# Numerators as 32x32 products, key-value sums in column tiles, and a layer norm by quarters in a four-layer attention kernel

## The chip, the cores and the metric

The kernel runs on one core of a Trainium2 chip. Its engines work side by side and meet through semaphores: TensorE multiplies matrices (PE in the profile; its loads of stationary matrices are PEld), VectorE (DVE) and ScalarE (ACT) work elementwise, GpSimd (POOL) does a little here, and SyncE (SP) mostly issues transfers. Products land in PSUM, eight banks of 512 fp32 columns over 128 partitions; everything else lies in SBUF.

The metric is the device time of one execution in microseconds, given as the median over the runs.

## The reference

Four layers follow each other: A, B, A, B, with the same weights for both A and both B. There are 2048 rows of 1024, and 32 heads of 32.

```
x = x + A(layernorm(x)); x = x + B(layernorm(x))      # and once more
A:  pq, pk = q @ w_phi, k @ w_phi                      # per head, 32x32
    phi_q = [softmax(pq), softmax(-pq)]                # 64 features per head, phi_k alike
    kv  = sum over s of phi_k[s,f] * v[s,d];  z = sum over s of phi_k[s,f]
    o   = (phi_q @ kv) / (phi_q @ z + 1e-6);  return o @ wo
B:  p = softmax(q k^T * 32**-0.5);  return (p @ v) @ wo
```

A is a linear attention: its keys are summed up once into a 32x32 matrix per head and sign, and its queries are multiplied with these. B is an ordinary attention over 2048 x 2048 scores per head.

## The kernel before

The activations stay in SBUF, transposed, as `xT`: 1024 features in eight blocks of 128 partitions, 2048 rows in four chunks of 512. Each pair of layers A and B is one turn of a loop (`layer` 0 and 1) with these stages:

- **Keys of A** (`a_keys`, L595 on). For each chunk: a layer norm (`layernorm`, L468 on), then for each half of the heads (`fc`) four blocks of 128 rows. A block has a product for the keys and one for the values, two exponentials (L615), their sums (L619), a reciprocal (L622), and the values multiplied by it into 33 columns per head, the last one holding the reciprocal itself (L628, L633). After four blocks the sums over rows follow (L647): for each of eight pairs of head group and sign, four products that contract the rows, with 128 stationary columns (four heads) and 132 moving ones (four heads of 33). Only the four diagonal blocks of 32x33 are wanted; they are added to an accumulator in SBUF by four DVE instructions for each of three banks of results (L662, L665).
- **State** (`a_state`). The accumulator is laid out for the queries: a block diagonal `kvm` of 128x128 per head group and sign, cleared by POOL (L688) and filled by four DVE copies (L692), and a matrix `zm` for the denominators from `zz` (L694, L700, L702).
- **Query pass of A** (`a_queries`, L734 on, and `a_out`). For each chunk and half: the query products, exponentials (L745), sums over features by small column tiles (L756), a correction of the negative half spread over heads by `spread` (L728, stationary `selb`), then for each of four head groups `a` the numerators (L783: two products of 128x128 by 512, for the two signs) copied out by ACT (L787), the denominators in column tiles (L794), their reciprocal by logarithm and exponential (L799, L801), spread again by `selb`, and multiplied in (L805). `a_out` multiplies by `wo` and adds to `xT` (L818). Then the chunk's layer norm for B follows, and B's keys of the first head group (`b_k`, evacuated at L841, moved by DMA at L834) and values.
- **Attention of B** (`attention`). Score products (L1009) use four row tiles of 32 partitions, three at a time into three banks; ACT takes the exponential of 1536 columns at once (L1017); the products with the values and with ones (L1047) use four column tiles. Some exponentials are made on DVE (L952 to L969). The projections of other head groups and the output projection run beside it as filler in bank 7 (L428), with column tiles. Towards the end of layer 0's attention the keys of layer 1's A for chunks 0 to 2 run there too (`alone`), with SBUF copies and bank 7 in place of free banks. Idle products (L1265) fill gaps.

The order of the work is not written out by hand. `Sched` collects every operation with its engine, an assumed duration, its dependencies, its buffers and a priority, then runs a list schedule over the engines and emits the instructions in that order; each engine's queue is in order. Buffers come from classes with a quota (`QUOTA`), and are given out in order of priority within a class; PSUM banks of class "num" have a quota of one. Each PE operation carries a mode that tells the array's shape: "n" for the whole array, "c" for column tiles, "r" for row tiles.

Layer norms outside attention square `xT` on ACT in two halves (L480), or in four quarters where `n=4`, and sum values and squares by products with a matrix of 1/1024 (L424); evacuations (L500, L502), the variance (L503), its logarithm and exponential (L505, L507) and four pairs of DVE instructions (L513, L517) follow. With two halves the squares and the sums wait for the whole chunk of `xT`; with quarters each waits for its two blocks. In the kernel before, only the first layer norm of layer 1 has `n=4`.

`gate` is an empty list: the first score product of an attention waits for its operands alone.

```
gate = []                                            # L1188
so = op("PE", 0.24, sfn, deps + (gate if n == 0 else []), ...)
```

Of the kernel before, what the change touches and what calls it, by code (L numbers as in the profile page):

```python
# [11 lines left out]
ALU = mybir.AluOpType  # L12
# [244 lines left out]
QUOTA = {"pk": 3, "pv": 2, "kv": 1, "ln": 2, "mm": 2, "cmp": 2, "bc": 4, "num": 1, "wt": 4, "fil": 2,  # L257
# [28 lines left out]
def kernel(  # L286
# [43 lines left out]
    selb = const.tile([P, P], BF16, tag="selb")  # L330
    fold = const.tile([P, DH], F32, tag="fold")
# [28 lines left out]
    )  # L360
    nc.vector.reduce_sum(out=hl[:], in_=fold[:, 4:8], axis=AX.X)
# [53 lines left out]
    def csl(c):  # L415
        return slice(c * C512, (c + 1) * C512)
# [50 lines left out]

    def layernorm(c, prio, banks, alone=False, n=2):  # L468
# [23 lines left out]
        m = mmgroup(mb, mv, lambda po: onesD[:], lambda po: xT[:, po, csl(c)], (), parts if n == 4 else [deps_x(c)] * 4, [], prio)  # L492
        q = mmgroup(qb, qv, lambda po: onesD[:], lambda po: xv()[:, po, :], [m],
# [34 lines left out]


# [65 lines left out]
    def a_keys(c, base, wk_s, wv_s, kv, banks, alone=False, step=0.1):  # L595
        xb, xv, fin = xnA[c]
        kv_b, kv_v, kv_last = kv
        for fc in range(2):
# [39 lines left out]
            for lo, hi in ((0, 3), (3, 6), (6, 8)):  # L638
                pr = base + step * (4 * fc + 3) + 1.5 * step
                pb, pv = ps("fil" if alone else "kv", banks)  # L640
                last = None
                for i in range(lo, hi):
                    gi, s = divmod(i, 2)

                    def fn(i=i, gi=gi, s=s, lo=lo, pv=pv, es=es, vs=vs):
                        for t in range(TB):
                            nc.tensor.matmul(  # L647
                                pv()[:, (i - lo) * 132:(i - lo + 1) * 132],
                                lhsT=es[t][1]()[:, s, gi * P:(gi + 1) * P],
                                rhs=vs[t][1]()[:, s, 4 * gi:4 * gi + 4, :].rearrange("p a b -> p (a b)"),  # L650
                                start=(t == 0), stop=(t == TB - 1))
                    last = op("PE", TB * 0.1, fn, [last] + flat([v[2] for v in vs]) + flat([e[2] for e in es]),
                              [pb] + [e[0] for e in es] + [v[0] for v in vs], pr, mode="n")
                adds = []
                for jj in range(4):
                    js = slice(32 * jj, 32 * jj + 32)
                    i0, i1 = 8 * fc + lo, 8 * fc + hi

                    def diag(pv=pv, js=js, jj=jj, n=hi - lo):
                        return pv()[js, 0:n * 132].rearrange("p (i x) -> p i x", x=132)[:, :, 33 * jj:33 * jj + 33]  # L660
                    if c == 0:
                        adds.append(op("DVE", dve_us(33 * (hi - lo)), lambda js=js, i0=i0, i1=i1, diag=diag: nc.vector.tensor_copy(  # L662
                            out=kv_v()[js, i0:i1, :], in_=diag()), [last], [pb, kv_b], pr))
                    else:
                        adds.append(op("DVE", dve_us(33 * (hi - lo)), lambda js=js, i0=i0, i1=i1, diag=diag: nc.vector.tensor_tensor(  # L665
                            out=kv_v()[js, i0:i1, :], in0=kv_v()[js, i0:i1, :], in1=diag(), op=ALU.add),
                            flat([last, kv_last.get((fc, lo))]), [pb, kv_b], pr))
                kv_last[(fc, lo)] = adds
# [13 lines left out]
    def a_state(kv, prio):  # L682
        kv_b, kv_v, kv_last = kv
        deps = flat(list(kv_last.values()))
        r = []
        m_b, kvm = sb("kvm", 16, P)
        z_b, zm = sb("zm", 16, DH)
        m0 = op("POOL", 2.0, lambda: nc.gpsimd.memset(kvm(), 0.0), (), [m_b], prio - 15)  # L688
        deps = deps + [m0]
        for j in range(4):  # L690
            js = slice(32 * j, 32 * j + 32)
            r.append(op("DVE", dve_us(512), lambda j=j, js=js: nc.vector.tensor_copy(  # L692
                out=kvm()[js, :, js], in_=kv_v()[js, :, 0:DH]), deps, [kv_b, m_b], prio))
        zs = [op("DVE", dve_us(16), lambda j=j: nc.vector.tensor_copy(  # L694
            out=zz[32 * j:32 * j + 32, :], in_=kv_v()[32 * j:32 * j + 32, :, DH]), deps, [kv_b], prio)
            for j in range(4)]
# [21 lines left out]
    def spread(r_b, r_v, dep, prio):  # L718

        got = []  # L720
        for a in (0, 2):
            bufs = [ps("bc", ANY) for _ in range(2)]
            bufs[0][0].with_ = (bufs[1][0],)

            def fn(a=a, bufs=bufs):
                for k in range(2):
                    rows = slice(32 * (a + k), 32 * (a + k) + 32)
                    nc.tensor.matmul(bufs[k][1](), lhsT=selb[rows, :], rhs=r_v()[rows, :],  # L728
                                     start=True, stop=True, tile_position=(32 * (a + k), 0))
            bm = op("PE", MM, fn, [dep], [bufs[0][0], bufs[1][0], r_b], prio, mode="r")  # L730
            got += [(b, v, bm) for b, v in bufs]
        return got

    def a_queries(c, hf, prio, wq_s, state, o_chunk):  # L734
# [37 lines left out]
        for a, (b_, v_, bm) in enumerate(spread(h_b, h_v, h, prio)):  # L772
# [4 lines left out]
        for a in range(4):  # L777
            g = 4 * hf + a
            n_b, n_v = ps("num", ANY)

            def fn(a=a, g=g, n_v=n_v):
                for s in range(2):
                    nc.tensor.matmul(n_v(), lhsT=kvm()[:, 2 * g + s, :], rhs=eq[a][1]()[:, s, :],  # L783
                                     start=(s == 0), stop=(s == 1))
            nm = op("PE", 2 * MM, fn, [ew[a]] + state, [n_b, m_b, eq[a][0]], prio, mode="n")
            s_b, s_v = sb("ns", C512, dt=F32)
            cp = op("ACT", act_us(512), lambda n_v=n_v, s_v=s_v: nc.scalar.copy(out=s_v(), in_=n_v()),  # L787
                    [nm], [n_b, s_b], prio)
            nums.append((s_b, s_v, cp))
# [14 lines left out]
        for a, (b_, v_, bm) in enumerate(spread(k_b, k_v, k, prio)):  # L804
# [330 lines left out]
    for layer in range(2):  # L1135
# [28 lines left out]
        wo_s = [slab("slab", second - 6 + fc, A_o[:, :, fc * C512:(fc + 1) * C512], C512) for fc in range(2)]  # L1164
# [10 lines left out]
        for c in range(NC):  # L1175
# [6 lines left out]
            xnB[c] = layernorm(c, pr + 23, ANY)  # L1182
# [5 lines left out]
        gate = []  # L1188
# [112 lines left out]
```

## Time and profile before

| | us |
|---|---|
| median of three runs | 2477.9 |
| the three runs | 2477.84, 2477.9, 2481.64 |
| span of the profiled execution (no other time is listed for it) | 2480.3 |
| PE busy | 2316.0 |
| ACT busy | 2131.0 |
| DVE busy | 1380.8 |

The mean granted clock of TensorE is 0.993 of full speed. The stages, read from the first and last instructions of their lines, are: start and folded key weights to about 60 us, keys of layer 0 to 197, its query pass to 371, attention to 1336, keys of chunk 3 in layer 1 to 1394, its query pass to 1571, attention to 2468, and the last projection to the end.

How to read the rows: a group row gives line, engine, operation, what it writes and reads, its shape and count, then busy time and the mean duration in ns, then the idle time before it with what ended it. A row of the timeline gives the start, the length, the same names and a count of instructions merged into it. "32*128" before a shape is the rows and columns of the array that a product uses. A row of SPq is the queue of SyncE as it issues a transfer.

### The profile page before, as it was taken

The numbers are of one execution on the slowest core, as the hardware profiler recorded it, in microseconds if no ns is written. First come the engines' busy times: TensorE is split into PE (matmuls) and PEld (weight loads), VectorE is DVE, ScalarE is ACT, GpSimd is POOL, SyncE is SP. The second block draws the span as 40 slices with busy tenths as digits, with TensorE's granted clock in tenths as the row PEclk, the third lists the DMA queues.
The fourth block names the chain that finished last, engine by engine and source line by source line (L and its number), as shares of the span: only waits on it lengthen the run. The fifth ranks groups of instructions, "written<-read, shape, count | busy, mean of one in ns | idle before, by whom it ended". The sixth has DMA issues, their size and how long they took to land. (4 is left out here: it accounts for less than half of the span.)

```text
span 2480.3 us, 61740 instructions
## 1 busy us (share of the span) xinstructions
PE 2316.0 (93%) x27084; PEld 870.4 (35%) x27084; DVE 1380.8 (56%) x1947; ACT 2131.0 (86%) x1887; POOL 24.9 (1%) x72
## 2 busy tenths in 40 slices
PE   7999999999999999999889999999999999998998
PEld 4443443333333333333333444333333333333333
DVE  6997653222266634543535766322255568789863
ACT  6335548999999999999997455699999999999998
POOL 0000000000000000000000000000000000000000
PEclk9999999999999999999999999999999999999999
DMA  9020011111121122213324001111121110110000
GB/s 219 24 56 1 6 38 40 43 36 45 39 66 42 47 66 70 78 50 86 120 57 128 1 5 30 31 39 43 41 61 34 31 30 29 32 32 27 27 25 32
DMA packets 204373, 118.32 MB, mean 48 GB/s; under 512 B 122440, under 2 KB 194120, under 8 KB 203336
## 3 DMA queue, kind: packets, MB, share of 16 engines
q1 hardware_dynamic: 203048, 112.29, 16.7%
q8 instruction: 211, 3.46, 0.6%
q10 hardware_dynamic: 1056, 2.10, 0.3%
q14 instruction: 58, 0.48, 0.1%
HBM read 78.71 MB, written 16.24 MB: 38 GB/s over the span
## 5 line engine op out<-in xcount | busy, mean ns | idle before, releaser
L1017 ACT ACTIVATE arena<-psum 128x1536 bf16<-128x1536 f32 x1332 | 1798.9, 1670 | 38.1 <-PE psum L1009 29.3
L1047 PE MATMUL psum<-arena 128*32 128x512 bf16 x4096 | 656.2, 388 | 7.3 <-DVE arena L1062 5.8
L1047 PE MATMUL psum<-arena,ones_bf 128*32 128x512 bf16 x4096 | 656.3, 388 | 0.0
L1009 PE MATMUL psum<-arena 32*128 32x512 bf16 x3996 | 525.0, 384 | 99.5 <-ACT arena L1017 91.1
L428 PE MATMUL psum<-arena 128*32 128x512 bf16 x8256 | 575.5, 381 | 5.4 <-DVE arena L612 1.9
L424 PE MATMUL psum<-arena 128*128 128x512 bf16 x2032 | 473.4, 382 | 17.0 <-ACT arena L745 3.2
L1009 PEld LDWEIGHTS <-arena 32*128 32x128 bf16 x3996 | 176.9, 91 | 620.6 <-issue 607.1
L424 PEld LDWEIGHTS <-arena 128*128 128x128 bf16 x2032 | 192.5, 98 | 265.4 <-issue 48.2
L428 PEld LDWEIGHTS <-arena 128*32 128x32 bf16 x8256 | 201.9, 96 | 214.8 <-issue 68.4
L1047 PEld LDWEIGHTS <-arena 128*32 128x32 bf16 x4096 | 158.0, 95 | 269.4 <-issue 238.6
L842 DVE CAST arena<-psum 128x512 bf16<-128x512 f32 x112 | 77.2, 690 | 255.2 <-PE psum L428 249.2
L966 DVE SCALAR_TENSOR_TENSOR arena<-arena 128x1024 f32<-128x1024 f32 x150 | 183.3, 1222 | 7.1 <-PE psum L1047 2.8
L1265 PE MATMUL psum<-xT,zero 128*32 128x512 bf16 x2172 | 171.7, 382 | 0.0
L1047 PEld LDWEIGHTS <-ones_bf 128*32 128x32 bf16 x4096 | 155.2, 95 | 18.7 <-issue 8.3
L1062 DVE COPY arena<-psum 128x512 f32<-128x512 f32 x126 | 86.5, 687 | 88.2 <-PE psum L1047 86.8
L615 ACT ACTIVATE arena<-psum 128x512 bf16<-128x512 f32 x80 | 42.7, 601 | 86.9 <-PE psum L424 57.5
L1103 DVE TENSOR_TENSOR arena<-arena 64x512 bf16<-64x512 f32 x124 | 84.7, 683 | 51.8 <-DMA arena<-rd 42.5
L952 DVE TENSOR_SCALAR arena<-psum 128x512 f32<-128x512 f32 x100 | 68.8, 688 | 67.7 <-PE psum L947 61.5
L745 ACT ACTIVATE arena<-psum 128x512 bf16<-128x512 f32 x128 | 69.8, 598 | 41.8 <-PE psum L424 32.0
L619 DVE TENSOR_REDUCE arena<-arena 128x32 f32<-128x1024 bf16 x64 | 77.7, 1214 | 41.2 <-ACT arena L615 34.0
L513 DVE TENSOR_TENSOR arena<-xT,arena 128x1024 f32<-128x1024 bf16 x64 | 78.0, 1219 | 35.9 <-ACT arena L502 34.7
L628 DVE TENSOR_TENSOR arena<-psum,arena 128x1024 bf16<-128x1024 f32 x64 | 77.7, 1215 | 30.0 <-PE psum L428 25.0
(100 smaller groups left out, 1394.5 us busy)
## 6 DMA issues: line engine op xcount, KB each, us to landing
arena<-rd SPq DMA_DIRECT2D x62, 256.0 KB
arena<-in_A_wqkv_dram SPq DMA_DIRECT2D x10, 1024.0 KB
arena<-in_B_wqkv_dram SPq DMA_DIRECT2D x32, 256.0 KB
arena<-arena SPq DMA_DIRECT2D x256, 32.0 KB
arena<-in_B_wo_dram SPq DMA_DIRECT2D x32, 256.0 KB
arena<-wd_k SPq DMA_DIRECT2D x8, 1024.0 KB
arena<-in_A_wo_dram SPq DMA_DIRECT2D x4, 1024.0 KB
arena<-in_B_wqkv_dram SPq DMA_DIRECT2D x4, 1024.0 KB
```

The source lines that it names most:

```text
L424: nc.tensor.matmul(out_, lhsT=lhsT, rhs=rhs, start=start, stop=stop, skip_group_check=True)
L428: nc.tensor.matmul(out_[ks, :], lhsT=lhsT[:, ks], rhs=rhs, start=start, stop=stop, tile_position=(0, 32 * k), skip_group_check=True)
L513: s1 = op("DVE", dve_us(1024), lambda pr=pr, w_v=w_v: nc.vector.tensor_tensor(out=w_v(), in0=xT[:, pr, csl(c)], in1=m_v().unsqueeze(1).to_ ...
L619: red = op("DVE", dve_us(1024), lambda ev=ev, sv=sv: nc.vector.reduce_sum(out=sv(), in_=ev().rearrange("p s (h d) -> p (s h) d", d=DH), ax ...
L628: ml = op("DVE", dve_us(1024), lambda vpv=vpv, wv_=wv_, sv=sv: nc.vector.tensor_tensor(out=wv_()[:, :, :, 0:DH], in0=vpv().rearrange("p (h ...
L966: last = [op("DVE", dve_us(1024), lambda i=i, c=c: nc.vector.scalar_tensor_tensor(out=x_v(), in0=(x_v() if i else g_v()), scalar=c, in1=g_ ...
L1009: nc.tensor.matmul(out=s_v()[:, x * C512:(x + 1) * C512], lhsT=kT[g][1]()[r, pp, d * P:(d + 1) * P], rhs=q_of[(qc, g)][1]()[r, (pp + j // ...
L1017: ex = op("ACT", act_us(w * C512), lambda s_v=s_v, e_v=e_v, w=w: nc.scalar.activation(out=e_v()[:, 0:w * C512], in_=s_v(), func=ACT.Exp, s ...
L1047: nc.tensor.matmul(out=a_v()[col:col + 32, :], lhsT=v_v()[:, kc % 4, o:o + DH] if what == 0 else ones_bf[:], rhs=ev()[:, x * C512:(x + 1) ...
L1062: cp = op("DVE", dve_us(512), lambda t_v=t_v, a_v=a_v: nc.vector.tensor_copy(out=t_v(), in_=a_v()), [last], [a_b, t_b], prio - 4)
L1103: s = [op("DVE", dve_us(512), lambda a=a, k=k, o_v=o_v, r_v=r_v, T=T: nc.vector.tensor_tensor(out=o_v()[a, :], in0=T[k][1]()[a, :], in1=r_ ...
L1265: nc.tensor.matmul(psum[32 * k:32 * k + 32, 6 * C512:7 * C512], lhsT=zero[:], rhs=xT[:, 0, 0:C512], start=False, stop=False, tile_position ...
```

## The change

Five things change together.

1. **Numerators.** `kvm` shrinks from 128x128 blocks to the 32x32 diagonal ones (`[128, 16, 32]`). A numerator for head group `a` is made of four 32x32 tiles per sign: head `j` of the group sits on partitions 32j and its result is written to partitions 32c with c = (j + a) mod 4. Two head groups go together into two banks (`NUMS` = 2), so that one operation has 16 products. Its mode is "s".
2. **Turned heads.** Since the results sit turned by `a`, the second `spread` takes a turned selection matrix `selr`, made at the start by 16 DVE copies of 32x32, and the slabs of `A_wo` are loaded with their rows turned alike (`slab_turned`): seven transfers per slab instead of one.
3. **Key-value sums.** For each pair of head group and sign, four column tiles of 32 stationary and 33 moving columns replace the product of 128 by 132. All eight pairs fit in one bank, 264 columns, and one DVE instruction over 128 partitions adds them to the accumulator. The assumed duration is `KVG`, the mode "c". The state is laid out by two DVE copies instead of eight, and without a clear.
4. **Layer norm.** The last layer norm of a query pass has four quarters (`LNN` = 4).
5. **Gate.** The first score product of each attention also waits for the mean products of that layer norm (`GATE`).

```diff
-QUOTA = {..., "num": 1, ...
+NUMS = 2
+LNN = 4
+GATE = (1, 1)
+KVG = 0.12
+QUOTA = {..., "num": NUMS, ...
...
+    for a in range(4):
+        for j in range(4):
+            c = (j + a) % 4
+            nc.vector.tensor_copy(
+                out=selr[32 * a:32 * a + 32, 32 * c:32 * c + 32], in_=selb[32 * a:32 * a + 32, 32 * j:32 * j + 32])
...
         m = mmgroup(mb, mv, lambda po: onesD[:], ...
+        lnq.append(m)
...
+    def slab_turned(cls, prio, src, n):
+        b, v = sb(cls, PO, n)
+        o = []
+        for a in range(4):
+            for lo, hi, to in ((0, P - 32 * a, 32 * a), (P - 32 * a, P, 0)):
+                if hi > lo:
+                    o.append(dma(prio, lambda a=a, lo=lo, hi=hi, to=to: nc.sync.dma_start(
+                        out=v()[to:to + hi - lo, a::4, :], in_=src[lo:hi, a::4, :]), (), [b], kb=2 * n * (hi - lo) / 512))
+        return b, v, [o] * 4
...
-            for lo, hi in ((0, 3), (3, 6), (6, 8)):
...
+            for i in range(8):
+                gi, s = divmod(i, 2)
...
                         for t in range(TB):
+                            for j in range(4):
+                                js = slice(32 * j, 32 * j + 32)
                                 nc.tensor.matmul(
-                                pv()[:, (i - lo) * 132:(i - lo + 1) * 132],
-                                lhsT=es[t][1]()[:, s, gi * P:(gi + 1) * P],
-                                rhs=vs[t][1]()[:, s, 4 * gi:4 * gi + 4, :].rearrange("p a b -> p (a b)"),
+                                pv()[js, i * 33:(i + 1) * 33],
+                                lhsT=es[t][1]()[:, s, gi * P + 32 * j:gi * P + 32 * j + 32],
+                                rhs=vs[t][1]()[:, s, 4 * gi + j, :],
+                                start=(t == 0), stop=(t == TB - 1), tile_position=(0, 32 * j), skip_group_check=True)
...
+                add = op("DVE", dve_us(264), lambda part=part, at_=at_: nc.vector.tensor_tensor(
+                    out=kv_v()[:, at_, :], in0=kv_v()[:, at_, :], in1=part(), op=ALU.add), ...
...
-        m0 = op("POOL", 2.0, lambda: nc.gpsimd.memset(kvm(), 0.0), (), [m_b], prio - 15)
...
-        for a in range(4):
-            g = 4 * hf + a
-            n_b, n_v = ps("num", ANY)
...
-                    nc.tensor.matmul(n_v(), lhsT=kvm()[:, 2 * g + s, :], rhs=eq[a][1]()[:, s, :], ...
+                    for k, (_, n_v) in enumerate(banks_):
+                        a = a0 + k
+                        for j in range(4):
+                            rows = slice(32 * j, 32 * j + 32)
+                            c = (j + a) % 4
+                            nc.tensor.matmul(
+                                n_v()[32 * c:32 * c + 32, :], lhsT=kvm()[rows, 2 * (4 * hf + a) + s, :],
+                                rhs=eq[a][1]()[rows, s, :], start=(s == 0), stop=(s == 1),
+                                tile_position=(32 * j, 32 * c), skip_group_check=True)
...
-        for a, (b_, v_, bm) in enumerate(spread(k_b, k_v, k, prio)):
+        for a, (b_, v_, bm) in enumerate(spread(k_b, k_v, k, prio, selr)):
...
-        wo_s = [slab("slab", second - 6 + fc, A_o[...], C512) for fc in range(2)]
+        wo_s = [slab_turned("slab", second - 6 + fc, A_o[...], C512) for fc in range(2)]
...
-            xnB[c] = layernorm(c, pr + 23, ANY)
+            xnB[c] = layernorm(c, pr + 23, ANY, n=LNN if c == NC - 1 else 2)
...
-        gate = []
+        gate = [lnq[-1]] if GATE[layer] else []
```

Since the schedule is made anew, the rest of the instructions is reordered too, above all the fillers beside attention.

More of the change, by code (lines that the diff above doesn't have):

```diff
@@ new lines, in part @@
+            def part(pv=pv):
+                return pv()[:, 0:8 * 33].rearrange("p (i x) -> p i x", x=33)
+            at_ = slice(8 * fc, 8 * fc + 8)
+            if c == 0:
+                add = op("DVE", dve_us(264), lambda part=part, at_=at_: nc.vector.tensor_copy(
+                    out=kv_v()[:, at_, :], in_=part()), [last], [pb, kv_b], pr)
+            else:
+                add = op("DVE", dve_us(264), lambda part=part, at_=at_: nc.vector.tensor_tensor(
+                    out=kv_v()[:, at_, :], in0=kv_v()[:, at_, :], in1=part(), op=ALU.add),
+                    [last, kv_last[fc]], [pb, kv_b], pr)
@@ L670, in mmg2 @@
+            kv_last[fc] = add
     def mmg2(pb, pv, lhs, rhs, d1, d2, bufs, prio, lo=0, hi=4, more=False):
@@ L771, in a_queries @@
         ew, nums = [], []
[L772 removed]
+        for a, (b_, v_, bm) in enumerate(spread(h_b, h_v, h, prio, selb)):
             ew.append(op("DVE", dve_us(512), lambda v_=v_, a=a: nc.vector.tensor_tensor(
```

74 lines of the change are left out of this document (29 added, 45 removed).

## The prediction, before the result was known

> **What bounds the kernel now.** I read the page first, then busy time by stage, then the groups by line, and last the instructions in order of time where stages meet.
>
> ```profile
> span 2480.3 us, 61740 instructions
> PE 2316.0 (93%) x27084; PEld 870.4 (35%) x27084; DVE 1380.8 (56%) x1947; ACT 2131.0 (86%) x1887; POOL 24.9 (1%) x72
> ```
>
> The shares are averages over stages with different limits, so they are split by stage. In the next view the columns are the stretch, its length, and busy time with count for PE, weight load, DVE, ACT, POOL.
>
> ```profile
> 60.00:197.00 137.00, 130.19 (x802) 65.12 (x801) 128.04 (x204) 47.33 (x87) 8.40 (x26) 1.00 0.14 42
> 197.00:220.20 23.20, 19.36 (x109) 6.86 (x107) 16.98 (x34) 14.88 (x28) 0.00 (x0) 1.00 0.00 1
> 265.00:311.40 46.40, 46.40 (x243) 19.29 (x242) 31.47 (x45) 26.46 (x44) 0.00 (x0) 1.00 0.03 7
> 395.00:1037.00 642.00, 608.48 (x8472) 213.07 (x8470) 267.06 (x367) 639.45 (x489) 2.62 (x8) 1.00 0.19 51
> 1037.00:1340.00 303.00, 273.14 (x3708) 101.67 (x3708) 130.66 (x212) 288.53 (x236) 6.89 (x17) 0.97 0.30 89
> 1393.00:1420.00 27.00, 22.50 (x121) 8.57 (x120) 19.18 (x39) 16.19 (x30) 0.00 (x0) 0.94 0.00 1
> 1593.30:2468.20 874.90, 820.08 (x11394) 283.75 (x11396) 516.44 (x667) 872.15 (x649) 0.00 (x0) 1.00 0.12 33
> ```
>
> Attention (rows 395 to 1340 and 1593 to 2468) is ACT's: it idles 2.6, 14.5 and 2.8 us there, and the change leaves its 1332 wide exponentials alone. A chunk of the query pass (row 265) is PE's to the last tenth. The keys of layer 0 (row 60) are shared: DVE 93%, PE 95%. So the change is paid where PE or DVE binds, in 0 to 395 and 1340 to 1593; what it does beside attention counts only inside the 14.5 us.
>
> **The numerators.** Rows of PE in order of time, then groups by line:
>
> ```profile
> 299.93 0.40 PE L728 MATMUL psum<-arena,selb 32*128 32x512 bf16 x4
> 315.54 0.60 PE L783 MATMUL psum<-arena 128*128 128x512 bf16 x2
> 316.07 0.61 PE L794 MATMUL psum<-arena 128*32 128x512 bf16 x8
> 316.62 0.61 PE L424 MATMUL psum<-arena 128*128 128x512 bf16 x2
> 91.60 0.86 PE L647 MATMUL psum<-arena 128*128 128x132 bf16 x12
> 92.30 1.03 PE L424 MATMUL psum<-arena 128*128 128x512 bf16 x4
> 2055.08 0.40 PE L428 MATMUL psum<-ident,xT 128*32 128x128 bf16 x16
> ```
> ```profile
> L783 PE MATMUL psum<-arena 128*128 128x512 bf16 x128 | 38.1, 379 | 2.1 <-ACT arena L787 1.7
> L647 PE MATMUL psum<-arena 128*128 128x132 bf16 x512 | 39.7, 223 | 7.8 <-DVE arena L665 6.1 <-DVE arena L628 1.4
> L665 DVE TENSOR_TENSOR arena<-arena,psum 32x99 f32<-32x99 f32 (+1 forms) x144 | 34.8, 242 | 19.6 <-PE psum L647 17.7
> L1062 DVE COPY arena<-psum 128x512 f32<-128x512 f32 x126 | 86.5, 687 | 88.2 <-PE psum L1047 86.8
> ```
>
> A duration holds the tail that the next product overlaps. L783 to L794, 0.53 us for two products, and L794 to L424, 0.55 us for eight column products, give 0.216 us for a full product, the same for four column tiles together, and 0.10 us for each change of array shape. L728 shows four row tiles together inside 0.40 us. Nothing shows 32x32 tiles. Bounds for a group of 16 over two banks: two slots, 0.43 us, if tiles that share neither rows and columns nor a bank region run together as L728's and L794's do; 16 slots, 3.46 us, if one after another. I take two, the nearest rows. Per pass 64 products, 13.8 us, become 512/2/8 = 32 slots, 6.9 us: -6.9. In the built order, from the first row sums to the last layer norm, shape changes go from 66 to 89 (layer 0) and 93 (layer 1): +2.3 and +2.7. Three score triples with their 0.65 us leave that stretch, since the gate holds them behind the means; 2 and 6 ordinary products enter it (+0.4, +1.3). A pass at 100% PE takes this one for one: -4.8 and -3.6, together **-8.4**.
>
> **The key-value sums.** A chunk and half had 32 products in about 32 x 0.058 = 1.84 us (0.70 us for twelve, L647 to L424). It gets 128 products in 32 groups of four column tiles. Nearest is the row with ident: sixteen 128-column products in 0.40 us, less the 0.22 of one, is 0.06 us per four. 33 columns can cost no more, and by columns 33/128 of it, 0.015. So 0.5 to 1.9 us, and 0.2 for two shape changes: between -1.15 and +0.27 per half-chunk. I take the upper end, since four weight loads go with each group and don't shrink: +0.27, for eight halves in layer 0 and two in layer 1 ahead of attention.
>
> The Trainium skill is harsher: "TensorE: Matmul & The Clock Gate", section "Wait — 56ns, not 53.3ns?", has start-to-start never under about 25 ns. The ident row disagrees (0.06/4 is 15 ns). By that figure the 128 products would be 3.2 us, an estimate from that page, and the sum 13 us higher.
>
> DVE's twelve adds per half, 12 x 0.242 = 2.9 us, become one of 264 columns: between 0.242 (99 columns) and 0.687 (512), by columns 0.42. That frees 2.5 us per half, seven times in row 60, or 17 of DVE's 128 us. PE then binds: 502 full products x 0.216, 224 x 0.058, 64 of the weight fold at about 0.056 and 1.3 of others make 126 us, with the sums' +1.9 now 128, of 137. The stage can shorten by 0 to 9 us; I take **-5**, half, since chunks wait for normed input in between. Layer 1 has one chunk: **+0.5**. Its last eleven adds and the state's copies (eight become two) no longer hold up the first numerators, but in the built order row sums now come behind the key-value products, and from row sums to numerators there is a chain over ACT and DVE. Of the idle PE in rows 197 and 1393 (3.8 and 4.5 us) I take **-2** for both.
>
> At the layer boundary, six half-chunks lie beside attention. PE and DVE have room there; the burst of 128 in bank 7 replaces three turns of that bank. ACT idles 14.5 us; I take **-2** (bounds -5 and +3). The cover is ACT's exponentials.
>
> **The last layer norm and the gate.**
>
> ```profile
> 369.15 0.69 DVE L818 TENSOR_TENSOR xT<-xT,psum 128x512 bf16<-128x512 bf16 x1 [1.04 <-PE psum L424]
> 369.48 1.45 ACT L1017 ACTIVATE arena<-psum 128x1536 bf16<-128x1536 f32 x1 [9.39 <-PE psum L1009]
> 370.83 3.70 ACT L480 ACTIVATE arena<-xT 128x2048 bf16<-128x2048 bf16 x2
> 374.43 0.59 ACT L500 ACTIVATE arena<-psum 128x512 f32<-128x512 f32 x1
> 374.58 1.02 PE L424 MATMUL psum<-arena,onesD 128*128 128x512 bf16 x4 [0.77 <-ACT arena L480]
> 375.52 1.23 DVE L513 TENSOR_TENSOR arena<-xT,arena 128x1024 f32<-128x1024 bf16 x1 [5.68 <-ACT arena L502]
> 376.66 0.69 DVE L503 TENSOR_TENSOR arena<-psum,arena 128x512 f32<-128x512 f32 x1
> 378.04 0.75 ACT L505 ACTIVATE arena<-arena,eps 128x512 f32<-128x512 f32 x1
> 378.82 0.63 ACT L507 ACTIVATE arena<-arena 128x512 f32<-128x512 f32 x1
> 379.36 5.45 ACT L1017 ACTIVATE arena<-psum 128x1536 bf16<-128x1536 f32 x4
> 385.41 1.22 DVE L517 TENSOR_TENSOR arena<-arena 128x1024 bf16<-128x1024 f32 x1
> 387.31 1.07 ACT L841 CAST arena<-psum 128x512 bf16<-128x512 f32 x2 [2.51 <-PE psum L424]
> 392.79 0.60 PE L1009 MATMUL psum<-arena 32*128 32x512 bf16 x6
> ```
>
> From the last residual add (end 369.84) to the score products that need the last key chunk (392.79) pass 23.0 us; ACT is continuous only from there. Afterwards three quarters of the squares run under the output projection, and 1.0 us (3.70/4 and its start) remains; two evacuations of the mean, 1.1; L513 and L503, 1.9; L505 and L507, 1.4: 5.5 us after the add. Seven exponentials stand next on ACT in the built order, 7 x 1.36 = 9.5, to 15.0; the norm on DVE (379.48 to 386.63 before, 7.2) and the last product are done at 13.3, so the evacuation waits till 15.0 and ends at 15.6. With 4.9 us from its end to the scores, as in 387.89 to 392.79, that is 20.5: **-2.5 per layer, -5**. Bounds: -4.2 without the seven ahead, and 0. The gate costs the two early exponentials their place under PE's work, 2.9 us, which the same interval absorbs: eight exponentials precede the last key chunk either way.
>
> **The start and the queues.**
>
> ```profile
> 1.20 0.47 DVE L343 MEMSET J_bf<- 32x32 bf16 x4
> 4.55 0.48 DVE L1117 MEMSET arena<- 128x512 uint32 x1
> 5.06 1.85 SPq L1118 DMA_DIRECT2D arena<-in_A_w_phi_dram  x4
> 6.95 8.95 SPq L459 DMA_TRANSPOSE xT<-in_A_x_dram  x7
> 33.09 1.91 ACT L480 ACTIVATE arena<-xT 128x2048 bf16<-128x2048 bf16 x1 [4.68 <-DMA xT<-in_A_x_dram]
> 164.71 0.37 SPq L525 DMA_DIRECT2D arena<-in_A_wo_dram  x1
> 223.18 1.27 DVE L818 TENSOR_TENSOR xT<-xT,psum 128x512 bf16<-128x512 bf16 x2
> ```
>
> Sixteen 32x32 copies for the turned matrix stand on DVE ahead of the clearing at 4.55. SP's queue waits for that clearing, and seven transposes of x wait behind it. At L343's 0.12 us each the start moves by **+1.9** (bounds 0, if PE's other work covers it, and 2.7). Each slab of A_wo becomes seven transfers instead of one, 24 more issues over both layers. In layer 0 the later slab was asked for at 164.71 and the projection's adds run at 223, so there is room; in layer 1 four of the first slab's stand between write and read-back of a denominator, which waits for its landing anyway: 0. If that cover were gone, six issues of about 0.5 us, 3 us, would show. POOL loses two clears nobody waits for.
>
> Sum: -8.4 -5 +0.5 -2 -2 -5 +1.9 = -20.0. The profiled execution's span of 2480.3 stands 2.4 us above the median of the runs, 2477.9; from the median, **2458 us**.
>
> **Rivals.** *Slower:* the row tiles of a group wait for one another because four of them write one bank. L728's tiles each have a bank of their own, so no row excludes it. Then 256 products per pass cost 55.3 instead of 6.9 us: +97, 2555 us. It decides from +0.63 us per group on (20 us over 32 groups). The Trainium skill, "TensorEngine Tiling (Array Packing)", section "Restrictions and Gotchas", says that different row tiles cannot access the same PSUM bank simultaneously; read strictly it means this rival. Against it: the four regions here are different partitions. Chance 0.09.
>
> *Four at a time:* two products share a row group with different moving data and don't overlap. Then the numerators gain nothing, +13.8: 2472 us. L794, four moving streams over all rows, speaks against it. 0.14.
>
> *Floor per product:* the small key-value products don't overlap at all. With 0.025 us each, between the ident row's 0.015 and L647's 0.058, ten half-chunks cost 13 more: 2471 us. 0.08.
>
> *The exponentials get in the way:* the seven ahead of the evacuation delay it until the layer norm gains nothing, and the two displaced ones per layer show: +5 and +5.8, 2469 us. For it: ACT is nearly full between 5.5 and 15.0. 0.09.
>
> **How the numbers follow.** Forecast 0.60; its own range is 2440 (keys -9, small products at 0.015, norm -4.2 each, boundary -5, start 0) to 2475 (keys, norm and state 0, boundary +3). The range 2440 to 2480 adds the middle rivals and leaves out the slow one and some tails. 0.2%, 5 us, is about what a measurement can tell: faster, under 2473: most of the forecast's 0.60 and two thirds of the 0.31: 0.78; same 0.10; slower 0.12.
>
> **What would show it.** Right: a group of 16 numerators followed 0.5 us later by the next work; 128 key-value products within 2 us; a keys stage near 132 us with DVE under 85%; scores of the last key chunk some 20 us after the last residual add; attention within 3 us of before. Wrong: 3 us for a numerator group, new ACT gaps at the layer boundary, or the x transposes late enough to move the whole start.

## The result and the profile after

The changed kernel takes **2448.4 us** (median of four runs, 2446.52 to 2449.21) against 2477.9 for the kernel before (four runs, 2475.13 to 2481.64). The ratio is 0.9875, 95% interval 0.9862 to 0.9889: 29.5 us less. The forecast was 2458 us, so the time lies inside the range, and the gain is half as large again as forecast. Between the two profiled executions the spans differ by 35.6 us: after's took 2446.52 us, 1.9 below its median and 1.8 above its span, and before's span alone lies 2.4 above the median. Terms read from the two traces therefore add up to 6 us more than the medians show.

The head of the page after:

```profile
span 2444.7 us, 65791 instructions
PE 2298.8 (94%) x29160; PEld 848.7 (35%) x29160; DVE 1337.6 (55%) x1775; ACT 2128.3 (87%) x1891; POOL 22.0 (1%) x70
```

2076 more products, 172 fewer DVE instructions, and no engine's share of the span has moved by more than a point. Where the time went is seen by stages. I cut both traces at the same pieces of work: the first multiplied values of the keys, the end of the 32nd such multiplication (keys), the end of the last residual add (query pass), the start of the ninth wide exponential (last layer norm), the end of layer 1's last key multiplication (attention with what runs beside it), the same three cuts in layer 1, and the last exponential. The stages in us, with the experiments told further down:

| | start | keys | query 0 | norm 0 | beside | query 1 | norm 1 | att. 1 | end | span |
|---|---|---|---|---|---|---|---|---|---|---|
| before | 38.1 | 150.9 | 180.9 | 23.4 | 993.1 | 183.5 | 23.5 | 874.8 | 12.1 | 2480.3 |
| after | 39.2 | 134.0 | 178.0 | 21.0 | 986.2 | 180.1 | 21.0 | 873.2 | 12.1 | 2444.7 |
| kv_alone | 38.4 | 133.7 | 182.1 | 23.4 | 980.4 | 181.5 | 23.5 | 874.5 | 12.1 | 2449.7 |
| kv_two_banks | 38.3 | 148.4 | 183.2 | 23.4 | 993.9 | 182.6 | 23.5 | 873.6 | 12.1 | 2479.0 |
| adds12 | 38.4 | 151.0 | 175.9 | 20.9 | 987.8 | 180.8 | 20.9 | 874.2 | 12.1 | 2462.0 |
| no_num | 37.7 | 134.1 | 182.2 | 21.0 | 992.2 | 181.8 | 21.0 | 874.2 | 12.0 | 2456.2 |
| kv_num | 38.7 | 133.3 | 178.6 | 31.7 | 989.7 | 180.1 | 32.8 | 875.4 | 12.1 | 2472.5 |
| no_gate | 38.6 | 135.7 | 178.8 | 20.6 | 984.9 | 179.7 | 20.6 | 874.9 | 12.1 | 2445.9 |
| gate_halves | 38.5 | 133.9 | 178.0 | 21.3 | 991.4 | 178.9 | 21.1 | 872.3 | 12.1 | 2447.5 |
| quarters_alone | 38.1 | 149.5 | 181.4 | 20.6 | 984.1 | 183.1 | 20.6 | 874.4 | 12.1 | 2463.9 |
| kv_quarters | 37.8 | 134.0 | 181.6 | 20.6 | 996.4 | 181.3 | 20.6 | 872.3 | 12.0 | 2456.6 |

Busy time in the first two stages and in the stretch beside attention, before (columns as in the prediction: stretch, length, PE, weight load, DVE, ACT, POOL):

```profile
38.10:189.00 150.90, 142.17 (x848) 70.32 (x847) 140.29 (x213) 56.22 (x93) 10.33 (x32) 0.99 0.29 69
189.00:369.80 180.80, 176.26 (x940) 73.64 (x939) 120.29 (x186) 97.23 (x163) 0.00 (x0) 1.00 0.06 15
393.30:1386.40 993.10, 927.88 (x12410) 335.73 (x12409) 436.37 (x629) 948.42 (x757) 12.10 (x33) 0.99 0.22 63
```

and after:

```profile
39.20:173.20 134.00, 132.06 (x1509) 64.53 (x1508) 122.37 (x136) 55.05 (x91) 10.35 (x32) 1.00 0.32 78
173.20:351.20 178.00, 174.51 (x1236) 68.32 (x1235) 116.24 (x169) 98.51 (x166) 0.00 (x0) 0.99 0.06 16
372.20:1358.40 986.20, 924.02 (x13223) 330.17 (x13222) 418.74 (x552) 946.70 (x755) 10.90 (x32) 0.99 0.22 63
```

The keys of layer 0 lost 16.9 us, nearly half of the whole: DVE fell from 93% to 91% of a shorter stage, and PE rose to 99%. The query passes lost 2.9 and 3.4, the two layer norms 2.4 and 2.5, the stretch beside attention 6.9, layer 1's attention 1.6; the start grew by 1.1. The experiments ask which edit each belongs to; the second table, behind them, shows what the granted clock took in each stage, and several of the smaller differences are its.

### The profile page after: what moved, and what is told of

It reads as the page before. It is cut to its first block, busy times and chain, and to the rows that moved or that the text cites. A ratio compares the mean times of both kernels' runs of the same rounds, so it can differ in the third digit from the quotient of the medians.

```text
span 2444.7 us, 65791 instructions
## 1 busy us (share of the span) xinstructions
PE 2298.8 (94%) x29160; PEld 848.7 (35%) x29160; DVE 1337.6 (55%) x1775; ACT 2128.3 (87%) x1891; POOL 22.0 (1%) x70
## 4 chain that ended last, share of the span: by engine, by line
ACT 43%; PE 35%; issue 10%; DVE 7%; DMA 3%; SPq 2%; ACTq 0%; DVEq 0%
ACT arena L1042 42%; PE psum L434 19%; PE psum L1072 5%; PE psum L438 4%; PE psum L1034 4%; DVE arena L991 2%; DMA arena<-rd 1%; SPq L469 1%; PE psum L1290 1%; DVE arena L1128 1%; ACT arena L638 1%; PE psum L804 1%; PE psum L671 1%; DVE arena L977 1%; DVE arena L1087 1%
## 5 line engine op out<-in xcount | busy, mean ns | idle before, releaser
L1290 PE MATMUL psum<-xT,zero 128*32 128x512 bf16 x2296 | 182.9, 380 | 0.0
```

The source lines that it names most:

```text
L1290: nc.tensor.matmul(psum[32 * k:32 * k + 32, 6 * C512:7 * C512], lhsT=zero[:], rhs=xT[:, 0, 0:C512], start=False, stop=False, tile_position ...
```

## The experiments

**The key-value sums alone.** Three explanations of the 16.9 us stood open. W: the work of the twelve adds on DVE bound the keys. B: PE waited for the single bank of the sums. P: the gain is one of the plan, which all five edits shape together. The first kernel is the one before with only the sums of the third part of the change (the state is laid out as before):

```diff
-            for lo, hi in ((0, 3), (3, 6), (6, 8)):     # 4 products of 128x132 a pair, 12 adds
+            for i in range(8):                          # 16 of 128x32 by 33 a pair, one bank
...
+                add = op("DVE", dve_us(264), ...)       # mode "c", KVG = 0.12
```

> The kernel before with the key-value sums of the change alone: column tiles of 33, one bank, one add per half-chunk; state, numerators, layer norm and gate stay as before. Theory W (the work of the twelve adds made DVE the bound of the keys, and PE waited) and theory B (PE waited for the single bank that the adds set free): both 2455 to 2463 us, keys of layer 0 some 13 us shorter, attention of layer 0 some 4 us shorter. Theory P (the gain comes from the plan that all five edits together happen to get): above 2467 us.

Measured: 2452.45 us, ratio 0.9900 [0.9879, 0.9920]. Its windows of keys and query pass:

```profile
38.40:172.10 133.70, 130.25 (x1491) 64.31 (x1505) 122.53 (x136) 55.09 (x91) 10.34 (x32) 1.00 0.33 78
172.10:354.20 182.10, 175.81 (x1031) 73.71 (x1049) 117.97 (x175) 98.47 (x165) 0.00 (x0) 0.99 0.06 15
```

The kernel is faster than either theory had, because the stretch beside attention is 12.7 us shorter, of which more below. The keys' whole gain is there, 17.2 us, with the old numerators and layer norms. P falls for the keys; W and B both stand. Two kernels tell them apart. One gives the sums of the kernel before a second bank:

```diff
-QUOTA = {..., "kv": 1, ...
+QUOTA = {..., "kv": 2, ...
```

> The kernel before with a quota of two banks in place of one for the key-value sums, and nothing else. Theory B: PE no longer waits for the adds, 7 to 10 us faster, 2468 to 2471 us. Theory W: DVE has the same work and PE waits for it elsewhere: within 3 us of before.

The other is the kernel after with its one add cut into twelve of 32 partitions, as before, while products and bank stay as they are:

```diff
-                add = op("DVE", dve_us(264), ...)
+            for lo, hi in ((0, 3), (3, 6), (6, 8)):
+                for jj in range(4):
+                    adds.append(op("DVE", dve_us(33 * (hi - lo)), ...))   # rows 32jj.., pairs lo..hi
```

> The changed kernel with the one add of 264 columns on 128 partitions cut into twelve of 32 partitions, as many and as wide as before; products and banks stay changed. Theory W: DVE gets back 2.5 us per half-chunk, keys of layer 0 8 to 14 us longer, 2456 to 2462 us. Theory B: the bank isn't needed again within the half, so at most 3 us slower, 2448 to 2451 us.

Measured: 2480.52 us for the second bank, ratio 1.0003 [0.9994, 1.0012], and 2463.66 for the twelve adds, 0.9934 [0.9918, 0.9950]. The keys window and the adds' group in the latter:

```profile
38.40:189.30 150.90, 141.14 (x1528) 67.12 (x1544) 141.84 (x217) 60.19 (x100) 10.36 (x32) 0.98 0.29 70
```
```profile
L694 DVE TENSOR_TENSOR arena<-arena,psum 32x99 f32<-32x99 f32 (+1 forms) x144 | 34.8, 242 | 6.6 <-PE psum L671 4.7
```

Twelve adds bring the stage back to 151.0 us, although the products are the cheap ones and the bank is one; some 3.4 us of that and 1.7 of the 150.9 before are the granted clock's, so the two agree to about 2 us. With a second bank the stage is 148.4 us, 2.5 shorter than before, and the query pass behind it is 2.3 longer (1.7 of each is the clock's). So W holds and B falls: the bank is worth about 1 us in the stage and nothing in the whole. Look at PE's column. It is 141.14 us "busy" in the stage with twelve adds, beside 132.06 for the same key products in the kernel after (some of the difference is query work that this plan had moved up into the stage, the count being 19 products higher, and up to 3.4 us is the clock). Before, it was 142.17. So part of the 94% of PE in this stage, 95% in the prediction's window, was waiting for DVE.

**The numerators taken out.** The kernel after, with the matrix, state, numerators and `wo` transfers of before:

```diff
-QUOTA = {..., "num": NUMS, ...        # kvm 32x32, selr, slab_turned
+QUOTA = {..., "num": 1, ...           # kvm 128x128, selb, slab
```

> The changed kernel with the numerators of before: whole-array products, unturned heads, block diagonal state, one transfer per slab of A_wo, no copies at the start. Numerators worth 3.5 to 5 us a pass, start worth -1: 2454 to 2458 us. Rival (stalls eat it): 2446 to 2450 us.

Measured: 2458.22, ratio 0.9908 [0.9892, 0.9924]. Against after, the query passes are 4.2 and 1.7 us longer and the start 1.5 shorter. The rest, 6 us, is in the stretch beside attention (992.2 against 986.2), where no numerator stands; 5.1 of it is the granted clock's by the second table. A kernel with the numerators alone on the kernel before gave no time.

**The layer norm and the gate.** First both were taken out of the kernel after:

```diff
-LNN = 4
-GATE = (1, 1)
+LNN = 2
+GATE = (0, 0)
```

> The changed kernel with the last layer norm by halves and no gate: key-value sums and numerators alone. Against the run with the key-value sums alone (2452.5 us): by the prediction the numerators take 3.5 to 5 us of PE from each query pass, less 1 to 2 at the start, 2443 to 2448 us. Rival (PE waits for ACT and DVE ahead of row sums and spreads, as much as the numerators save): 2451 to 2455 us.

Measured: 2472.65, ratio 0.9970 [0.9960, 0.9980], which neither theory had. Both layer norms became 8 and 9 us longer than in the kernel before, 31.7 and 32.8 us. The layer boundary of that kernel, in order of time:

```profile
349.93 0.69 DVE L843 TENSOR_TENSOR xT<-xT,psum 128x512 bf16<-128x512 bf16 x1 [1.04 <-PE psum L434]
351.61 3.70 ACT L492 ACTIVATE arena<-xT 128x2048 bf16<-128x2048 bf16 x2
355.21 8.14 ACT L1042 ACTIVATE arena<-psum 128x1536 bf16<-128x1536 f32 x6
358.22 0.39 PE L1034 MATMUL psum<-arena 32*128 32x512 bf16 x3
360.72 0.39 PE L1034 MATMUL psum<-arena 32*128 32x512 bf16 x3 [0.18 <-ACT arena L1042]
362.24 1.90 PE L434 MATMUL psum<-xT,onesD 128*128 128x512 bf16 x8
```

The last residual add is done at 350.62 and the squares at 355.3 (351.61 + 3.70), but the eight products that average the values start at 362.24, and those that average the squares come behind them: PE's queue is in order, and score triples stand ahead of them, which go at the pace of the exponentials that empty their banks. That gave a theory O (the order: what costs is score products ahead of the means, and either edit prevents it) against Q (the quarters do it). Two kernels, each with one of the two edits:

```diff
 LNN = 4
-GATE = (1, 1)
+GATE = (0, 0)                         # no_gate
```

> The changed kernel without the gate; the layer norm stays by quarters. By the prediction the gate costs and gives nothing by itself, eight exponentials fit ahead of the last key chunk either way: 2446 to 2451 us. Rival (without the gate score products and exponentials stand ahead of squares and means, and the quarters' gain is lost): the stretch from the last residual add to the ninth exponential 23 us again in both layers, 2452 to 2455 us.

```diff
-LNN = 4
+LNN = 2                               # gate_halves
 GATE = (1, 1)
```

> The changed kernel with the last layer norm by halves as before, and the gate kept. Theory O (the 21 us that the version without both loses come from the order: score products take six banks and PE's turn ahead of the mean products; either the gate or the quarters prevent it): the means come right after the last residual add, the ninth exponential 23 to 24 us after it, 2451 to 2456 us. Theory Q (the quarters themselves are worth it, since the squares then run under the output projection): 31 us again, 2468 to 2473 us.

Measured: 2448.50 (0.9878 [0.9861, 0.9895]) without the gate, 2449.39 (0.9875 [0.9858, 0.9891]) without the quarters: neither differs from after. The layer norms take 20.6 and 20.6 us, and 21.3 and 21.1. The boundary with the gate and halves, in order of time:

```profile
348.83 3.71 ACT L492 ACTIVATE arena<-xT 128x2048 bf16<-128x2048 bf16 x2 [11.74 <-PE psum L434]
349.50 1.89 PE L434 MATMUL psum<-xT,onesD 128*128 128x512 bf16 x8
353.39 2.80 ACT L1042 ACTIVATE arena<-psum 128x1536 bf16<-128x1536 f32 x2
```

Here the squares are no longer behind an early exponential (the kernel before had one there, at 369.48; here ACT stands waiting for 11.74 us and takes the squares next), and the means start with them. O holds, Q falls, although O had expected 23 to 24 us: the two edits are two ways to the same 2.5 us per layer, and together they give no more.

The quarters alone on the kernel before:

```diff
-            xnB[c] = layernorm(c, pr + 23, ANY)
+            xnB[c] = layernorm(c, pr + 23, ANY, n=4 if c == NC - 1 else 2)
```

> The kernel before with the last layer norm of a query pass by quarters and nothing else, no gate. The prediction's step: 2.5 us per layer, 20.5 us from the last residual add to the scores of the last key chunk in place of 23.0, 2472 to 2476 us. Rival (the plan lets exponentials ahead of the squares): no gain or a loss, 2477 us and above.

Measured: 2464.12, ratio 0.9936 [0.9921, 0.9950], more than expected. The layer norms gained 2.8 and 2.9 us, a little more than forecast; 9.0 us more are in the stretch beside attention, which no line of this edit touches. Is that an effect of the quarters, or of the plan (S: each edit makes the schedule anew, and the stretch takes what it takes)? The quarters on top of the key-value sums decide it, without numerators and gate:

```diff
 # kv_alone
-            xnB[c] = layernorm(c, pr + 23, ANY)
+            xnB[c] = layernorm(c, pr + 23, ANY, n=4 if c == NC - 1 else 2)
```

> The run without the new numerators, now also without the gate: key-value sums and quarters on the kernel before. Theory S (what happens beside attention of layer 0, from the tenth exponential to the last keys of layer 1, is a matter of the plan and belongs to no edit): keys 133.5 to 134.5 us, the stretch from the last residual add to the ninth exponential 20.5 to 21 us, both as in the run without numerators, but the stretch beside attention anywhere in 978 to 991 us, so 2446 to 2458 us. Rival (it belongs to the edits: the numerators' removal made it 990): 990 again, 2457 to 2459 us.

Measured: 2459.21, ratio 0.9917 [0.9902, 0.9931]: slower than kv_alone by 6.8 us, with 2.8 and 2.9 us gained in the layer norms. The stretch beside attention in kv_alone and in kv_quarters:

```profile
377.60:1358.10 980.50, 922.36 (x13229) 329.51 (x13232) 418.74 (x552) 946.70 (x755) 12.62 (x33) 1.00 0.22 63
```
```profile
374.00:1370.40 996.40, 933.94 (x13271) 330.50 (x13270) 418.27 (x552) 948.55 (x755) 12.54 (x33) 0.98 0.22 63
```

The same edit gave -9.0 there on one kernel and +16.0 on the other, with the same work of ACT and DVE to 2 us. So the stretch's share of a difference belongs to no edit, as S has it, although 996.4 lies outside the 978 to 991 that S allowed. But the reason for most of it is not the plan. The granted clock, third number from the right, is 1.00 in the first row and 0.98 in the second.

**What the granted clock took.** The clock recorded in each trace is at full speed except in pieces of 3.4 us, sometimes 6.8, at half speed. One piece of kv_quarters with the stretch ahead of it, then one of the kernel after, with the products that ran into it:

```profile
724.80:728.20 3.40, 0.87 (x15) 0.38 (x7) 3.32 (x6) 2.69 (x3) 0.00 (x0) 1.00 0.00 0
728.20:735.00 6.80, 6.80 (x54) 1.44 (x50) 3.31 (x5) 5.00 (x5) 0.00 (x0) 0.50 0.01 1
```
```profile
197.30:200.70 3.40, 1.64 (x9) 0.69 (x10) 2.88 (x6) 1.62 (x4) 0.00 (x0) 0.99 0.02 5
200.70:204.10 3.40, 3.40 (x9) 1.09 (x8) 3.12 (x6) 0.63 (x1) 0.00 (x0) 0.50 0.00 0
200.03 5.59 PE L434 MATMUL psum<-arena 128*128 128x512 bf16 x17 [0.22 <-DVE arena L830]
```

Seventeen products took 5.59 us, where 16 x 0.216 and the last one's 0.38 are 3.84: the piece cost 1.7 us, half of its length. Ahead of it PE was busy for 1.64 of 3.40 us, and ahead of the other for 0.87. The same holds for all 119 pieces of the fourteen traces: in the 3.4 us ahead of each, PE was busy for at most 70% of the time. Half of the half-speed time is therefore an estimate of what the clock took. In us, by stage (0 in the layer norms, but 3.4 and 1.7 in those of kv_num):

| | keys | query 0 | beside | query 1 | att. 1 |
|---|---|---|---|---|---|
| before | 1.7 | 0 | 8.5 | 1.7 | 3.4 |
| after | 0 | 1.7 | 5.1 | 3.4 | 1.7 |
| kv_alone | 0 | 1.7 | 1.7 | 0 | 3.4 |
| kv_two_banks | 0 | 1.7 | 10.2 | 0 | 1.7 |
| adds12 | 3.4 | 1.7 | 6.8 | 1.7 | 3.4 |
| no_num | 0 | 1.7 | 10.2 | 1.7 | 3.4 |
| quarters_alone | 0 | 1.7 | 3.4 | 1.7 | 3.4 |
| kv_quarters | 0 | 0 | 15.4 | 0 | 0 |

Without these the stretch beside attention, 980 to 996 us as measured, is 979 to 985 us in all fourteen traces: 984.6 before, 981.1 after, 978.7 in kv_alone, 981.0 in kv_quarters. Of the 6.9 us between before and after, 3.4 are the clock's by this estimate, and of the 9.0 of quarters_alone 5.1. It can also account for the 6.8 us between the medians: the runs of kv_alone had mean clocks of 0.993 to 0.997, those of kv_quarters 0.990 to 0.994, and kv_alone itself took 2457.82 us at 0.993 and 2451.43 at 0.997. How far the plan, which places the holes in PE's work, and how far chance decides on these pieces is not shown; one kernel's runs differ by as much.

**The start.** The sixteen copies of the turned matrix are put behind the clearing that SP's queue waits for:

```diff
-    for a in range(4): ...                # 16 copies, ahead of everything
+    turned = op("DVE", 2.0, turn, [phi_0], (), -19.9)
```

> The changed kernel with the sixteen copies for the turned matrix after the clearing for the phi loads in place of before it; nothing else. By the prediction the start gets back 1 to 2 us, 2446 to 2447.5 us, with the first multiplied values as early as before (38.1 us). Rival (the start is hidden by PE's other work): the same as the changed kernel, 2448 us.

Measured: 2447.20, ratio 0.9869 [0.9854, 0.9883]; the start is 38.3 instead of 39.2 us, 0.9 of the expected 1 to 2, and the difference of 1.2 us to after is less than the runs can tell. Two more kernels varied that one. The first changes only a duration that the scheduler assumes, which gives the same instructions in another order:

```diff
 # late_turn
-KVG = 0.12
+KVG = 0.17
```

> The changed kernel with the copies for the turned matrix behind the phi clearing, and the planned duration of eight column groups at 0.17 in place of 0.12 us (the trace has 0.13): the same instructions, another plan. By the theory that the keys, the query pass and the chain to the last key chunk are set by DVE and PE work, these stay within 1.5 us of the version with 0.12; beside attention the plan may move the time by up to 6 us either way, as between the earlier runs: 2441 to 2453 us.

The second leaves the gate out:

```diff
 # late_turn
-GATE = (1, 1)
+GATE = (0, 0)
```

> The changed kernel with the copies behind the phi clearing and without the gate, quarters kept. By the runs so far the gate is not needed beside quarters: 2445 to 2449 us, the same as the changed kernel less about 1 us for the start. Rival: the plan puts score products ahead of the means again, 2465 us and above.

Measured: 2448.81 (0.9870 [0.9855, 0.9885]) and 2448.48 (0.9879 [0.9862, 0.9895]). Neither differs from after, and I found no version that clearly beats it.

## Why the prediction was right, and where its sizes were off

The direction, the mechanisms and the time were right within the range. Of the sizes, one large term failed, and the others came out near, most of them once the granted clock is accounted for.

**Keys of layer 0: -5 forecast, -16.9 measured; the step that failed.** It named the right resource (the 2.5 us per half that come free on DVE; adds12 shows it) and mis-sized twice. The price of 128 small products was taken at the upper of its bounds, because "four weight loads go with each group and don't shrink". One such sum on PE after, in order of time, and then the groups of the products and the add:

```profile
125.03 1.20 PE L671 MATMUL psum<-arena 128*32 128x33 bf16 x128
126.16 8.38 PE L434 MATMUL psum<-arena 128*128 128x512 bf16 x38
```
```profile
L671 PE MATMUL psum<-arena 128*32 128x33 bf16 x2048 | 20.7, 183 | 0.3 <-DVE arena L651 0.3
L686 DVE TENSOR_TENSOR arena<-arena,psum 128x264 f32<-128x264 f32 x12 | 5.1, 426 | 14.5 <-PE psum L671 14.5
```

1.13 us to the next work, and 0.10 for the change of shape ahead: 1.23 against 1.84 before, so -0.6 per half-chunk instead of +0.27. The single add is 0.426 us, as the 0.42 worked out. With -0.6 for +0.27, PE's bill of 128 of 137 us would have read 122, and the gain 0 to 15. The second slip was to halve it, "since chunks wait for normed input". Counted by slots, PE's work was 135.8 of 150.9 us before (550 full products of 0.216, 224 of 0.058, 64 of 0.056, and 0.4) and 129.7 of 134.0 after (547 full ones, seven sums of 1.13, the same 64). So PE stood, waited or ran at half speed for 15 us before and for 4 after: little was left waiting for normed input. The prediction's own bill, 126 of 137 us, already held 11 such us; they came free with DVE's, and half of them were given away. DVE's busy time in the stage fell by 17.9 us and the stage by 16.9 (15.2 without the clock's 1.7). The sign named, DVE under 85%, did not come, since the stage shrank with DVE's work: 91%.

**Numerators: -8.4 forecast, -4.2 and -1.7 measured beside no_num, some -4.2 and -3.4 without the clock.** The price was right:

```profile
285.12 0.62 PE L804 MATMUL psum<-arena 32*32 32x512 bf16 x16
285.68 0.60 PE L434 MATMUL psum<-arena 128*128 128x512 bf16 x2
```

Sixteen products in 0.56 us, two slots and a change of shape, where 0.53 was worked out. The rivals *slower* (3.46 us a group) and *four at a time* fall with this row. The Trainium skill, "TensorEngine Tiling (Array Packing)", section "Restrictions and Gotchas", which spoke for *slower*, has it that different row tiles cannot use one bank at the same time; the trace does not agree: here four of them wrote four quarters of one in those 0.56 us. But the pass, as measured, shortened by less than forecast. From the first to the last numerator of layer 0, before and after:

```profile
L783 PE MATMUL psum<-arena x64: 376/379/389, 199.1 to 354.1; 128*128 128x512 bf16 x64
```
```profile
L804 PE MATMUL psum<-arena x256: 372/383/386, 182.2 to 334.2; 32*32 32x512 bf16 x128
```

155.0 against 152.0, and in layer 1 155.7 against 154.3. Holes in PE's work are not the reason: by the rows of the query pass above they are 4.5 us before (180.80 - 176.26) and 3.5 after. Nor are there more changes of shape than forecast: counted in the traces they went from 66 to 90 and from 68 to 94, close to the 89 and 93 that the built order had. Most of it is the clock. By the second table it took 0 and 1.7 us of the query passes before, 1.7 and 3.4 after, 1.7 and 1.7 in no_num. Without these, after's query passes are 176.3 and 176.7 us and no_num's 180.5 and 180.1: by this estimate 7.6 us of the 8.4 came, and a pass at 100% PE does take the gain nearly one for one.

**The last layer norm: -5 forecast, -4.9 measured**, and by the steps written down. The boundary after, in order of time:

```profile
350.49 0.69 DVE L843 TENSOR_TENSOR xT<-xT,psum 128x512 bf16<-128x512 bf16 x1 [1.04 <-PE psum L434]
354.31 1.45 ACT L1042 ACTIVATE arena<-psum 128x1536 bf16<-128x1536 f32 x1 [0.95 <-PE psum L1034]
355.65 0.71 ACT L518 ACTIVATE arena<-arena,eps 128x512 f32<-128x512 f32 x1
356.40 0.63 ACT L520 ACTIVATE arena<-arena 128x512 f32<-128x512 f32 x1
356.93 9.48 ACT L1042 ACTIVATE arena<-psum 128x1536 bf16<-128x1536 f32 x7
366.24 0.65 ACT L866 CAST arena<-psum 128x512 bf16<-128x512 f32 x1
371.69 0.60 PE L1034 MATMUL psum<-arena 32*128 32x512 bf16 x6
```

Add done at 351.18, seven exponentials in 9.48 us ahead of the evacuation, scores at 371.69: 20.5 us, the number forecast. The rival *exponentials in the way* falls: they set the 20.5, and do not eat the gain. What the prediction did not see is that quarters and gate are substitutes; it gave the gate no time, which is right beside the quarters only. One reason is that with halves the squares and the sums do not wait for the whole chunk, as was said of the kernel before: in the rows of gate_halves above they start at 348.83 and 349.50, and the last residual add ends at 350.4. The plan alone assumes that wait.

**The small terms.** The start: +1.9 forecast, +1.1 measured; copies take 0.10 us each, not 0.12 (1.64 for sixteen), and the clearing moved from 4.55 to 5.20. That 0.65 is nearer to the copies' part: the kernels of the table with them start at 38.4 to 39.2 us, those without at 37.7 to 38.4. The turned `wo` slabs cost nothing visible, as forecast. Beside attention: -2 (bounds -5 and +3) against -6.9, outside the bounds; without the clock's 3.4 it is -3.5, inside them. A bound from the idle time of ACT left out that PE's clock changes the stretch by more than that. Attention of layer 1 took 1.6 us less, which is the clock's 1.7. State and transition, -2 for both layers, lie in the query rows above and were not measured apart; the whole query stage went by -2.9 and -3.4 (-4.6 and -5.1 without the clock), against the -4.8 and -3.6 of the numerators alone. The *floor per product* falls: 1.13 us for 128 products, not 3.2.

Without the key term the forecast was, by the stages as measured, 4.1 us too hopeful in the query passes and state (-10.4 against -6.3) and 4.9 too cautious beside attention, which cancels; without the clock these are 0.7 and 1.5. What is left of the miss is the keys: 11.9 of the 15.6 us by which the two spans differ more than forecast; between the medians the miss is 9.5 us.

## What to carry to other kernels

When two engines are both above 90% in a stage, take the work of one away in thought and ask whether the other's "busy" would stay: the twelve narrow adds here stretched PE's time as well as DVE's, and one wide instruction paid for both. A short chain at the border of two stages is protected by order: look for products that may run early, take banks, and stand ahead of the chain in a queue; either the work that feeds the chain comes earlier, or the early work is held back, and one of the two is enough. In a kernel whose schedule is made anew at every edit, measure an edit on two base kernels before crediting it with a stretch that it does not touch, and compare the granted clock of each stage before explaining a few us in it.

## What the runs showed of the hardware that was not expected

- A product of 128 rows by 32 stationary and 33 moving columns costs 8 ns when four column tiles take turns: (1.20 - 0.185)/31 is 0.033 us for each four, half of what 128 moving columns cost in the ident row (15 ns), four weight loads included. The Trainium skill, "TensorE: Matmul & The Clock Gate", section "Wait — 56ns, not 53.3ns?", has at least 25 ns from start to start; these rows do not agree with it as a figure per instruction, though 33 ns for each column tile would.
- An add over 32 partitions by 99 columns takes 253 ns by itself (the 242 of the row is a mean with adds of 66 columns), one over 128 partitions by 264 columns 426 ns: some eleven times the elements for 1.7 times the time.
- Behind 3.4 us in which TensorE was at most 70% busy, its clock was halved for the next 3.4 or 6.8 us, at 119 places in fourteen traces; where TensorE was the bound, about half of that time was lost (1.7 us in the rows above). Whether every such hole is followed by one is not shown.
- Score products that were allowed to run early made two layer norms 10.4 and 11.7 us longer (31.7 and 32.8 in kv_num against 21.3 and 21.1 in gate_halves), of which 3.4 and 1.7 are the clock's. Even without these that is more than any of the layer norm's own operations lasts.
